# Two attentions and a feed-forward: maxima written in PSUM, work moved between the heads

## The chip, the cores and the metric

The kernel runs on one core of one Trainium2 chip as one program. The metric is the device time in microseconds from start to end of that program. The core has five engines with a queue of instructions each: TensorE (PE in the profile; its weight loads are PEld), VectorE (DVE), ScalarE (ACT), GpSimd (POOL) and SyncE (SP), which here only issues DMAs. They wait for each other by semaphores. TensorE writes to PSUM, a small memory of eight banks; the other engines read it from there into SBUF.

## The reference

Three stages follow each other, all in float32, with 4 batches, 576 positions and 512 features:

```python
# 1. attention with decay: 8 heads of 64 for each batch
cum = cumsum(log(clip(f, 1e-4, 1)), -1)
scores = q @ k.T / 8 + (cum[..., :, None] - cum[..., None, :])     # masked above the diagonal
attn = exp(scores - max(scores)); attn /= attn.sum(-1) + 1e-9
x = heads_side_by_side(attn @ v)                                   # (4, 576, 512)
# 2. mixing of positions by rank 32, and a feed-forward 512 -> 2048 -> 512
u = x + (x.T @ U @ V).T
y = u + relu(u @ w_ch1) @ w_ch2
# 3. four experts, each a masked attention of width 64; two of them count at each position
logits = y @ w_gate
w = softmax(the two largest logits)
out = sum over e of (w[e] if e is chosen else 0) * (softmax(causal((y wq[e]) (y wk[e]).T / 8)) @ (y wv[e]) @ wo[e])
```

## The kernel before

Nearly all products are made of a high and a low part: each operand is split into a rounded part (names that end in `h`, or `qa`, `ka`) and the rest (`l`, `qb`, `kb`), and three matmuls are added in PSUM. In the first attention a pair of heads shares its loads, so there are 16 pairs, four to a batch; the heads are counted 0 to 31 here. In the second attention a head is one expert of one batch, 0 to 15.

One head is made in these turns. `scores` (L186) makes the transposed scores in two parts, `sc`, each in a PSUM buffer of two banks; ScalarE takes the exponential into `pf` and a 16-bit `ph`, and VectorE the rest `pl`. So that the exponentials cannot overflow, the maximum of each row goes into the scores as an additional row of the matmul, and it is made before, for a later head: `row_max` (L148) has three turns. The first multiplies the last fifth of the rows, `ua`, and VectorE takes the masked maximum of 576 columns (L157), which adds the mask, writes the sum to `junk` in SBUF and the maximum to `mx`. The second does the same with the other four fifths, `ub` (448, 320, 192 and 64 columns, L175). `sc`, `ua` and `ub` share two buffers (tag `s2`). The third turn transposes the maxima on TensorE, `mt` (L180), VectorE scales them to `mr` (L182), and two DMAs on SP's queue write them into row 66 of `qa`. `weighted_values` makes `av` from `ph`, `pl` and the values, `normalise` scales it (L285). The values are scaled first by a power of two from their largest magnitude: `am` on VectorE (L249), `amt` on TensorE, `rsp`, `rs`.

The 16 tiles of the first two quarters of the feed-forward weights come in during the first attention. Each is a DMA, three steps on VectorE that narrow 64-bit numbers (L306, L308, L309, to `wst`), one on ScalarE between them (L307), the high part on ScalarE and the low part on GpSimd. `WRATE` says how many tiles are asked for behind each pair; their order on the engines is then set by the scheduler. `GROUPS` says how many pieces of feed-forward stand in each pair.

TensorE's order is written by hand: `first_batch` (the first four pairs), `later_batches` (the other twelve) and the loop of the second attention run turns of Python generators one after the other, `one(gen)` being one turn. The other engines' order comes from the scheduler. In the second attention the filling stands in a list `work` of generators, and `work_on(n)` takes n pieces from its front: `experts_qk` (projections of two experts: four pieces of 12 matmuls `pq`, L848), `expert_values` (five pieces of 12 matmuls `pv`, L891, then `am` and the scale, and the gates: `eq` and others on VectorE), `expert_out` (two pieces of transposes `op`, five of 6 matmuls `po`, L934) and `last_out` for the last batch. In a head stand, in this order: the first part of the scores, `ua` of the head after the next, one piece, the second part, one piece, `ub`, one piece, the weighted values of the head before, two pieces, `mt`, and in most heads another piece (none in the last batch but for its last head).

Of the kernel before, what the change touches and what calls it, by code (L numbers as in the profile page):

```python
# [8 lines left out]
F32 = mybir.dt.float32  # L9
# [8 lines left out]
P = 128  # L18
# [3 lines left out]
E = 4  # L22
# [13 lines left out]
PSCALE = 256.0  # L36
VEXP = 8192.0

WRATE = (0, 1, 2, 3, 3, 3, 2, 2)
GROUPS = (0,) * 5 + (6, 6, 7) + (8,) * 7 + (3,)  # L40
BIG = -1.0e30
NEG = -3.0e38
ISC = 0.125
# [13 lines left out]
def kernel(  # L57
# [90 lines left out]
    def row_max(hb, mx, apart=False):  # L148


        qa, qb, ka, kb = hb
        ua = ps2.tile([P, 2, 512], F32, name="ua", tag="s2")
        for c0, c1 in ((0, HC), (HC, S)):
            nc.tensor.matmul(ua[:, c0 // HC, 0:HC], qa[0:66, M_LO[4]:S], ka[0:66, c0:c1],
                             start=True, stop=True)
        junk = cur["att"].tile([P, S], BF16, name="junk", bufs=1)
        nc.vector.tensor_tensor_reduce(  # L157
            junk[:].rearrange("p (c n) -> p c n", c=2), ua[:, :, 0:HC],
            maskm[:].rearrange("p (c n) -> p c n", c=2), 1.0, NEG, OP.add, OP.max, mx[:, 4:5])
        if apart:  # L160
            yield
        ub = ps2.tile([P, 2, 512], F32, name="ub", tag="s2")
        where = {3: (0, 0), 0: (0, 448), 2: (1, 0), 1: (1, 320)}
        for t in (3, 2, 1, 0):
            bk, off = where[t]
            w = M_W[t]
            n = 64 if t == 0 else P
            nc.tensor.matmul(ub[0:n, bk, off:off + w], qa[0:66, M_LO[t]:M_LO[t] + n],  # L168
                             ka[0:66, 0:w], start=True, stop=True)
        for t in (3, 2, 1, 0):  # L170
            bk, off = where[t]
            w = M_W[t]
            n = 64 if t == 0 else P
            m0 = S - P if t == 0 else S - w
            nc.vector.tensor_tensor_reduce(  # L175
                junk[0:n, 0:w], ub[0:n, bk, off:off + w], maskm[0:n, m0:m0 + w], 1.0, NEG,
                OP.add, OP.max, mx[0:n, t:t + 1])
        yield
        mt = psf.tile([NT, P], F32, name="mt", tag="f")
        nc.tensor.transpose(mt[:], mx[:], ident[:])  # L180
        mr = small.tile([NT, P], F32R, name="mr", bufs=2)
        nc.vector.tensor_scalar(mr[:], mt[:], PSCALE_LN / ISC, None, OP.subtract)  # L182
        row = f32(qa[66:67, :])
        nc.sync.dma_start(row[:, 0:64], f32(mr[0:1, 0:64]))
        cur["last"] = nc.sync.dma_start(row[:, 64:S].rearrange("o (t p) -> o t p", p=P),
                                        f32(mr[1:NT, :]))  # L186
# [343 lines left out]
    def maxima(p, j, apart=False):  # L530
        if p < NPAIR:
            yield from row_max(pair_heads(p)[j], next_mx(), apart)

    def one(gen):

        next(gen, None)
# [104 lines left out]
    def pair_scores(p, j):  # L641
        st_p[p, j] = yield from scores(pair_heads(p)[j])

    def first_batch(m_next):

        mixing = vals = iter(())
        for h in range(2 * NP):
            p, j = divmod(h, 2)  # L650
            sc = pair_scores(p, j)
            one(sc)
            one(m_next)
            m_next = maxima(p + 1, j, True)
            one(m_next)
            if j == 0:
                xs[p] = sx.tile([P, NT, P], F32, name="x", bufs=2)
                vals = values(p + 1)
                one(vals)
            one(sc)  # L660
            if j == 1:
                next_inputs(p + 2)
            one(m_next)
            if j == 1:
                one(vals)
            if h > 0:
                attend(*divmod(h - 1, 2))
            if j == 0:
                one(vals)
                one(mixing)  # L670
            elif p > 0:
                mixing = mix(p - 1)
                one(mixing)
            if j == 1:
                weights_after(p)
        one(mixing)
        return m_next

    def later_batches(m1):

        m0 = iter(())
        for p in range(NP, NPAIR):
            some = [1] * GROUPS[p]

            def group():
                if some:
                    fill(some.pop())

            xs[p] = sx.tile([P, NT, P], F32, name="x", bufs=2)
            if p == NP:
                cur["att"] = att
            vals = values(p + 1)
            mixing = mix(p - 1)
            sc = pair_scores(p, 0)
            one(sc)
            group()
            one(m1)
            one(sc)  # L700
            group()
            m0 = maxima(p + 1, 0)
            one(m0)
            group()
            attend(p - 1, 1)
            one(vals)
            group()
            sc = pair_scores(p, 1)
            one(sc)
            one(vals)  # L710
            group()
            one(m0)
            one(mixing)
            one(sc)
            next_inputs(p + 2)
            group()
            one(mixing)
            if p == NP:
                sin0.release()
                att0.release()  # L720
                pre.release()
                cur["fu"] = pool("fu", 2, "right")
                cur["fh"] = pool("fh", 8, "right")
                cur["fy"] = pool("fy", 3, "right")
            if p % NP == 0:
                ffn_prepare(p - NP)
                if p == NP:
                    ffn_prepare(1)
            m1 = maxima(p + 1, 1)
            one(m1)  # L730
            one(vals)
            group()
            attend(p, 0)
            group()
            weights_after(p)
            fill(len(some))
        attend(NPAIR - 1, 1)
        fill(1)
        drain(mix(NPAIR - 1))
        ffn_prepare(NPAIR - NP)  # L740
# [232 lines left out]

    def expert_attend(b, e):
        if e == 0:
            st_o[b] = sy.tile([P, NT, E * D], F32, name="o3")
        vh, vl, rs, cf = st_v[b]
        ph, pl = st_e[b, e]
        av = weighted_values(ph, pl, vh[:, :, e], vl[:, :, e])
        rn = row_scales(av, rs, cf[:, e, :])  # L980
        normalise(st_o[b][:, :, e * D:e * D + D], av, rn)
# [9 lines left out]
    def work_on(n):  # L991

        while n and work:
            if next(work[0], 1) is None:
                n -= 1
            else:
                work.pop(0)

    NH = B * E
    with tc.manual_schedule(engines={mybir.EngineType.PE}):  # L1000
        drain(experts_qk(0, 0, y))
        work.append(experts_qk(0, 1, y))
        work_on(2)
        m0, m1 = head_max(0), head_max(1)
        one(m0)
        work_on(1)
        one(m0)
        work_on(1)
        one(m1)
        work.append(expert_values(0, y))  # L1010
        work_on(1)
        one(m1)
        work_on(1)
        one(m0)
        work_on(3)
        one(m1)
        y_next = load_y(1, ys[1], sy, "yst")
        for h in range(NH):
            b, e = divmod(h, E)
            more = b + 1 < B  # L1020
            if e == 0 and more:
                y = y_next
                work.append(experts_qk(b + 1, 0, y))
            if e == 1 and b + 2 < B:
                with tc.issue_after(cur["last"].ins):
                    y_next = load_y(b + 2, ys[b % 2], sy, "yst")
            if e == 1 and b > 0:
                work.append(expert_out(b - 1))
            if e == 2 and more:
                work.append(experts_qk(b + 1, 1, y))  # L1030
            if e == 3 and more:
                work.append(expert_values(b + 1, y))
            if e == 3 and not more:
                tail = last_out(b)
                work.append(tail)
            sc = expert_scores(b, e)
            m = head_max(h + 2) if h + 2 < NH else iter(())
            one(sc)
            one(m)
            work_on(1)  # L1040
            one(sc)
            work_on(1)
            one(m)
            work_on(1)
            if h > 0:
                expert_attend(*divmod(h - 1, E))
            work_on(2)
            one(m)
            if b == B - 1:
                work_on(e == 3)  # L1050
            elif e < 3:
                work_on(1)
        expert_attend(B - 1, E - 1)
        work_on(100)
    for p_ in (ys[1], sy, att, hpool2, hpool, sy0, sw, small, psf, ps1, ps2, dram, const):
# [58 lines left out]
```

## Time and profile before

| | |
|---|---|
| median of 3 runs | 966.55 us (965.96, 966.55, 969.4) |
| profiled execution | 971.0 us, its span 969.1 |
| TensorE busy | 862.1 us, 89% (7480 matmuls); weight loads 808.2 |
| VectorE busy | 568.4 us, 59% |
| ScalarE, GpSimd busy | 416.7 us, 293.5 us |
| granted TensorE clock, mean | 0.93 |
| moved by DMA | 101.94 MB |

The profile gives an engine's busy time in the whole span; the stages have different limits. TensorE is busy in nine tenths and more of nearly every slice between 130 and 720 us, where the feed-forward stands, and less at both ends. "Windows" cut the span into stretches and give each engine's busy time in them, and the clock that TensorE was granted, 1.00 being 2.4 GHz and 0.50 being 1.2 GHz. A wait in the profile is put down to the instruction that released it last.

### The profile page before, as it was taken

The page shows a single profiled execution, that of the slowest core. Times are in us where ns is not written, and L with a number is a line of the kernel's source. Part 1 is how long each engine was busy: PE and PEld are TensorE (multiplying, and loading weights), DVE is VectorE, ACT ScalarE, POOL GpSimd, SP SyncE. Part 2 cuts the span into 40 slices and gives each one's busy share as a digit, 9 for nine tenths or more (in the row PEclk, how much of TensorE's full clock was granted, in tenths as well). Part 3 has the DMA queues.
Part 4 walks back from the last instruction along what each step waited for, and adds up shares of the span by engine and source line. Part 5 has one row for each costly group of instructions (what it writes and reads, how often), then busy time and mean ns, then how long its engine had stood idle before and what let it go on. Part 6 is the DMA issues. An engine that isn't in the chain of part 4 may idle for free.

```text
span 969.1 us, 19020 instructions
## 1 busy us (share of the span) xinstructions
PE 862.1 (89%) x7480; PEld 808.2 (83%) x7480; DVE 568.4 (59%) x1468; ACT 416.7 (43%) x808; POOL 293.5 (30%) x262
## 2 busy tenths in 40 slices
PE   2769778878999998999999999999999797989887
PEld 2758667777899998989998999999999786878775
DVE  6787767776576665652246653222225778576654
ACT  4656446445545444441233342322113455545543
POOL 8444444433242223121225342423014132110000
PEclk9985559888999998999999999999999999999968
DMA  6344453335333232203158763423113213212111
GB/s 176 109 133 139 123 179 89 111 88 168 119 108 99 78 107 81 65 26 110 50 168 305 230 216 110 147 72 108 46 61 99 70 43 80 67 23 74 31 45 55
DMA packets 68777, 101.94 MB, mean 105 GB/s; under 512 B 6608, under 2 KB 49424, under 8 KB 68688
## 3 DMA queue, kind: packets, MB, share of 16 engines
q1 hardware_dynamic: 64416, 92.47, 32.6%
q10 hardware_dynamic: 4272, 8.26, 2.3%
q8 instruction: 59, 0.97, 0.4%
q14 instruction: 30, 0.25, 0.1%
HBM read 60.33 MB, written 22.56 MB: 86 GB/s over the span
## 4 chain that ended last, share of the span: by engine, by line
PE 68%; DVE 13%; DMA 8%; ACT 4%; issue 3%; POOL 2%; SPq 1%; ACTq 0%; POOLq 0%; DVEq 0%
PE cps L384 18%; PE hps L369 18%; PE sc L211 9%; PE pq L848 3%; PE po L934 3%; DMA ust<-udram 3%; PE pv L891 3%; PE av L238 3%; DVE pl L222 3%; PE ub L168 2%; PE gp L551 2%; PE av L242 2%; PE av L240 2%; DVE junk L175 2%; DMA vr<-in_v_dram 1%
## 5 line engine op out<-in xcount | busy, mean ns | idle before, releaser
L384 PE MATMUL cps<-hh,w2h 128*128 128x288 f32 x512 | 156.0, 305 | 5.2 <-DVE yc L386 3.9
L369 PE MATMUL hps<-uh,w1h 128*128 128x288 f32 x512 | 145.5, 305 | 8.8 <-ACT uh L354 8.8
L222 DVE TENSOR_TENSOR pl<-pf,ph 128x576 f16<-128x576 f32 x144 | 125.2, 874 | 47.0 <-ACT ph L221 46.7
L384 PE MATMUL cps<-hh,w2l 128*128 128x288 f32 x512 | 152.5, 298 | 0.0
L384 PE MATMUL cps<-hl,w2h 128*128 128x288 f32 x512 | 151.7, 296 | 0.0
L374 DVE SCALAR_TENSOR_TENSOR hl<-hps,hh 128x288 fp32r<-128x288 f32 x128 | 58.3, 455 | 145.7 <-ACT hh L373 145.4
L369 PE MATMUL hps<-uh,w1l 128*128 128x288 f32 x512 | 142.2, 299 | 0.0
L373 ACT ACTIVATE hh<-hps 128x288 fp32r<-128x288 f32 x128 | 52.4, 409 | 165.3 <-PE hps L369 165.0
L369 PEld LDWEIGHTS hps<-uh,w1h 128*128 128x128 f32 x512 | 98.0, 191 | 9.5 <-ACT uh L354 9.3
L220 ACT ACTIVATE pf<-sc 128x576 f32<-128x576 f32 x144 | 83.4, 612 | 47.9 <-PE sc L211 41.9
L384 PEld LDWEIGHTS cps<-hh,w2h 128*128 128x128 f32 x512 | 97.5, 191 | 6.5 <-DVE yc L386 4.6
L369 PEld LDWEIGHTS hps<-uh,w1l 128*128 128x128 f32 x512 | 98.2, 192 | 0.0
L384 PEld LDWEIGHTS cps<-hh,w2l 128*128 128x128 f32 x512 | 97.4, 190 | 0.0
L384 PEld LDWEIGHTS cps<-hl,w2h 128*128 128x128 f32 x512 | 97.3, 190 | 0.0
L238 PE MATMUL av<-vh,ph 128*128 128x65 f16 x720 | 92.8, 208 | 1.5 <-DVE x L285 1.5
L369 PE MATMUL hps<-ul,w1h 128*128 128x288 f32 x512 | 90.3, 299 | 3.3 <-POOL ul L355 3.3
L240 PE MATMUL av<-vl,ph 128*128 128x64 f16 x720 | 91.5, 204 | 0.0
L242 PE MATMUL av<-vh,pl 128*128 128x65 f16 x720 | 91.3, 204 | 0.0
L221 ACT CAST ph<-pf 128x576 f16<-128x576 f32 x144 | 88.5, 638 | 1.6
L211 PE MATMUL sc<-qa,ka 67*128 67x288 f32 (+4 forms) x288 | 81.2, 343 | 8.2 <-ACT pf L220 4.3
L175 DVE CUSTOM_DVE_ANT_0 junk<-ub,maskm 128x448 bf16<-128x448 f32 x192 | 79.7, 415 | 12.1 <-PE ub L168 10.7
L355 POOL TENSOR_TENSOR ul<-ust,uh 128x1152 fp32r<-128x1152 f32 x22 | 58.7, 2670 | 82.9 <-ACT uh L354 82.8
(160 smaller groups left out, 2002.4 us busy)
## 6 DMA issues: line engine op xcount, KB each, us to landing
raw<-in_w_dram SPq DMA_DIRECT2D x32, 512.0 KB
ust<-udram SPq DMA_DIRECT2D x22, 576.0 KB
qkt<-in_qk_dram SPq DMA_DIRECT2D x16, 576.0 KB
yc<-ydram SPq DMA_DIRECT2D x14, 576.0 KB
ydram<-yc SPq DMA_DIRECT2D x14, 576.0 KB
vr<-in_v_dram SPq DMA_DIRECT2D x16, 320.0 KB
udram<-ustage ACTq DMA_DIRECT2D x16, 288.0 KB
ydram<-ust SPq DMA_DIRECT2D x8, 576.0 KB
```

The lines of the kernel that those rows point to most:

```text
L175: nc.vector.tensor_tensor_reduce(junk[0:n, 0:w], ub[0:n, bk, off:off + w], maskm[0:n, m0:m0 + w], 1.0, NEG, OP.add, OP.max, mx[0:n, t:t + 1])
L211: nc.tensor.matmul(ps[:, bk, off:off + w], wa, xa, start=bk not in banks[:n], stop=bk not in banks[n + 1:])
L220: nc.scalar.activation(pfv, view, AF.Exp, scale=ISC)
L221: nc.scalar.copy(ph[:, o0:o0 + n], pf[:, 0:n])
L222: nc.vector.tensor_tensor(pl[:, o0:o0 + n], pf[:, 0:n], ph[:, o0:o0 + n], OP.subtract)
L238: nc.tensor.matmul(av[0:m, it, :], ph[0:k, c:c + m], vh[0:k, jt, :], start=first, stop=False)
L240: nc.tensor.matmul(av[0:m, it, 0:64], ph[0:k, c:c + m], vl[0:k, jt, :], start=False, stop=False)
L242: nc.tensor.matmul(av[0:m, it, :], pl[0:k, c:c + m], vh[0:k, jt, :], start=False, stop=last)
L355: nc.gpsimd.tensor_tensor(ul[:], ust[:], f32(uh[:]), OP.subtract)
L369: nc.tensor.matmul(ph[:], wa[:, k, fs], xa[:, k, :], start=n == 0, stop=n == 3 * KT - 1)
L374: nc.vector.scalar_tensor_tensor(hl[:], ph[:], 0.0, f32(hh[:]), OP.max, OP.subtract)
L384: nc.tensor.matmul(pc[:], wa[:, t, dsl], xa[:], start=n == 0, stop=n == 3 * FT - 1)
```

## The change

- The maxima's masked sums, which nothing reads, are written back to the place in PSUM that they are read from (`ua`, `ub`); the tile `junk` is gone.
- First attention, first batch: the third turn of the maxima (`mt`, `mr`, the row's DMAs) stands behind the second part of the scores and no longer in front of `ua`. In the other twelve pairs it stands behind the second part of the scores and a group of feed-forward in both heads, where it stood in front of the second part.
- The weights' tiles behind the pairs are 0, 0, 1, 4, 4, 4, 3 and not 0, 1, 2, 3, 3, 3, 2, 2.
- Second attention: the values of the next batch are put in the list in expert 1, not 3, the second half of the projections at the front of it in expert 2; the outputs of batches 0, 1 and 2 are put in from head 9 on, not one batch later each. How many pieces stand in front of `mt` in each head is in a table, `PIECES`, and behind `mt` none. The attention's results `o3` have three buffers, where they had two.

```diff
--- before.py
+++ after.py
@@ -36,8 +36,10 @@
 PSCALE = 256.0
 VEXP = 8192.0
 
-WRATE = (0, 1, 2, 3, 3, 3, 2, 2)
+WRATE = (0, 0, 1, 4, 4, 4, 3)
 GROUPS = (0,) * 5 + (6, 6, 7) + (8,) * 7 + (3,)
+
+PIECES = (3, 2, 2, 2) + (1,) * 4 + (3,) * 4 + (2, 2, 2, 3)
 BIG = -1.0e30
 NEG = -3.0e38
 ISC = 0.125
@@ -153,9 +155,8 @@
         for c0, c1 in ((0, HC), (HC, S)):
             nc.tensor.matmul(ua[:, c0 // HC, 0:HC], qa[0:66, M_LO[4]:S], ka[0:66, c0:c1],
                              start=True, stop=True)
-        junk = cur["att"].tile([P, S], BF16, name="junk", bufs=1)
         nc.vector.tensor_tensor_reduce(
-            junk[:].rearrange("p (c n) -> p c n", c=2), ua[:, :, 0:HC],
+            ua[:, :, 0:HC], ua[:, :, 0:HC],
             maskm[:].rearrange("p (c n) -> p c n", c=2), 1.0, NEG, OP.add, OP.max, mx[:, 4:5])
         if apart:
             yield
@@ -173,7 +174,7 @@
             n = 64 if t == 0 else P
             m0 = S - P if t == 0 else S - w
             nc.vector.tensor_tensor_reduce(
-                junk[0:n, 0:w], ub[0:n, bk, off:off + w], maskm[0:n, m0:m0 + w], 1.0, NEG,
+                ub[0:n, bk, off:off + w], ub[0:n, bk, off:off + w], maskm[0:n, m0:m0 + w], 1.0, NEG,
                 OP.add, OP.max, mx[0:n, t:t + 1])
         yield
         mt = psf.tile([NT, P], F32, name="mt", tag="f")
@@ -649,15 +650,15 @@
         for h in range(2 * NP):
             p, j = divmod(h, 2)
             sc = pair_scores(p, j)
+            m_last, m_next = m_next, maxima(p + 1, j, True)
             one(sc)
-            one(m_next)
-            m_next = maxima(p + 1, j, True)
             one(m_next)
             if j == 0:
                 xs[p] = sx.tile([P, NT, P], F32, name="x", bufs=2)
                 vals = values(p + 1)
                 one(vals)
             one(sc)
+            one(m_last)
             if j == 1:
                 next_inputs(p + 2)
             one(m_next)
@@ -696,9 +697,9 @@
             sc = pair_scores(p, 0)
             one(sc)
             group()
-            one(m1)
             one(sc)
             group()
+            one(m1)
             m0 = maxima(p + 1, 0)
             one(m0)
             group()
@@ -709,11 +710,11 @@
             one(sc)
             one(vals)
             group()
-            one(m0)
             one(mixing)
             one(sc)
             next_inputs(p + 2)
             group()
+            one(m0)
             one(mixing)
             if p == NP:
                 sin0.release()
@@ -973,7 +974,7 @@
 
     def expert_attend(b, e):
         if e == 0:
-            st_o[b] = sy.tile([P, NT, E * D], F32, name="o3")
+            st_o[b] = sy.tile([P, NT, E * D], F32, name="o3", bufs=3)
         vh, vl, rs, cf = st_v[b]
         ph, pl = st_e[b, e]
         av = weighted_values(ph, pl, vh[:, :, e], vl[:, :, e])
@@ -1024,12 +1025,14 @@
             if e == 1 and b + 2 < B:
                 with tc.issue_after(cur["last"].ins):
                     y_next = load_y(b + 2, ys[b % 2], sy, "yst")
-            if e == 1 and b > 0:
-                work.append(expert_out(b - 1))
+            if e == 1 and more:
+                work.append(expert_values(b + 1, y))
+            if e == 1 and b == 2:
+                work.append(expert_out(0))
+            if e < 2 and b == 3:
+                work.append(expert_out(1 + e))
             if e == 2 and more:
-                work.append(experts_qk(b + 1, 1, y))
-            if e == 3 and more:
-                work.append(expert_values(b + 1, y))
+                work.insert(0, experts_qk(b + 1, 1, y))
             if e == 3 and not more:
                 tail = last_out(b)
                 work.append(tail)
@@ -1044,12 +1047,9 @@
             work_on(1)
             if h > 0:
                 expert_attend(*divmod(h - 1, E))
-            work_on(2)
+
+            work_on(PIECES[h])
             one(m)
-            if b == B - 1:
-                work_on(e == 3)
-            elif e < 3:
-                work_on(1)
         expert_attend(B - 1, E - 1)
         work_on(100)
     for p_ in (ys[1], sy, att, hpool2, hpool, sy0, sw, small, psf, ps1, ps2, dram, const):
```

TensorE in head 0 of the first attention, from the end of the first part of the scores on; `identb` and `maskt` are the causal mask. Before:

```order
L211 LDWEIGHTS identb
L211 MATMUL sc<-maskt,identb 128x128
L180 MATMUL mt<-ident,mx_96 5x128 [waits DVE_49]
L154 MATMUL ua<-ka_154,qa_152 128x288 [waits Activation_49]
L154 MATMUL ua<-ka_154,qa_152 128x288
L211 MATMUL sc<-qa_136,ka_138 128x320 [waits Activation_49]
```

and with the change, the same place and the end of the second part:

```order
L212 LDWEIGHTS identb
L212 MATMUL sc<-maskt,identb 128x128
L156 MATMUL ua<-ka_154,qa_152 128x288 [waits DVE_49,Activation_49]
L156 MATMUL ua<-ka_154,qa_152 128x288
L212 MATMUL sc<-qa_136,ka_138 128x320 [waits Activation_49]
...
L212 MATMUL sc<-maskt,identb 128x128
L181 MATMUL mt<-ident,mx_96 5x128
L169 MATMUL ub<-ka_154,qa_152 128x448 [waits DVE_49]
```

`mt` has moved behind the ten matmuls and four masks of the second part and waits for nothing of its own; the wait for VectorE stands at `ua`.

VectorE in head 4 of the first attention, where `wst` is a weight's tile, `g` the mixing, `am` the values' magnitude and `den` a head's sums. Before:

```order
L306 TENSOR_SCALAR wst<-raw 128x512
L555 TENSOR_TENSOR g<-gp,g 32x128
L182 TENSOR_SCALAR mr<-mt 5x128
L157 ISA junk,mx_98<-ua,maskm 128x576
L157 ISA mx_98 128x1
L308 SCALAR_TENSOR_TENSOR wst<-raw,wst 128x512
L222 TENSOR_TENSOR pl<-pf,ph 128x576
L309 SCALAR_TENSOR_TENSOR wst<-raw,wst 128x512
L249 TENSOR_REDUCE am<-vr 128x1
L175 ISA junk,mx_98<-ub,maskm 128x448
```

and with the change:

```order
L286 TENSOR_TENSOR x<-av,rn 128x5x64
L556 TENSOR_TENSOR g<-gp,g 32x128
L158 ISA ua,mx_98<-ua,maskm 128x2x288
L158 ISA mx_98 128x1
L223 TENSOR_TENSOR pl<-pf,ph 128x576
L183 TENSOR_SCALAR mr<-mt 5x128
L176 ISA ub,mx_98<-ub,maskm 128x448
```

The three `wst` steps are gone from between the maxima, `mr` stands behind the maximum of `ua`, and `am` (in the next rows) behind the first maximum of `ub`.

TensorE in head 12 of the second attention, from the end of its weighted values on. Before:

```order
L240 MATMUL av<-vl_10785,ph 128x64
L242 LDWEIGHTS pl
L242 MATMUL av<-vh_10784,pl 128x65
L180 MATMUL mt<-ident,mx_98 5x128
L211 MATMUL sc<-qa_8040,ka_8042 128x288
```

and with the change:

```order
L935 MATMUL po<-wol,oh 128x512
L935 MATMUL po<-woh,ol 128x512
L935 MATMUL po<-woh,oh 128x512
L935 MATMUL po<-wol,oh 128x512
L935 MATMUL po<-woh,ol 128x512
L181 MATMUL mt<-ident,mx_98 5x128
L212 MATMUL sc<-qa_8008,ka_8010 128x288
```

Output products (two pieces of six matmuls, the end of which is shown) now stand between the weighted values and `mt`, where nothing stood.

## Rows read from the trace of the kernel before

**Rows 1.** Windows, first attention; columns: length, busy time (instructions), granted clock, DMA.

```profile
18.97:40.73 21.76, 14.60 (x95) 12.79 (x96) 16.07 (x40) 12.73 (x23) 10.70 (x11) 1.00 0.46 132
40.73:46.46 5.73, 5.51 (x74) 4.98 (x72) 4.70 (x16) 4.07 (x8) 3.73 (x3) 1.00 0.02 5
46.46:64.69 18.23, 14.29 (x163) 12.33 (x160) 14.31 (x40) 10.68 (x19) 10.66 (x7) 0.91 0.61 183
64.69:79.62 14.93, 10.58 (x82) 9.30 (x81) 13.33 (x37) 8.79 (x16) 6.16 (x6) 0.67 0.37 106
79.62:90.54 10.92, 10.14 (x79) 9.07 (x78) 7.79 (x25) 6.37 (x12) 5.45 (x4) 0.52 0.39 109
90.54:105.57 15.03, 11.24 (x88) 9.58 (x87) 12.56 (x29) 8.12 (x15) 5.76 (x4) 0.71 0.61 180
105.57:130.78 25.21, 22.27 (x158) 18.86 (x158) 15.87 (x41) 14.24 (x26) 9.51 (x7) 0.50 0.44 119
```

**Rows 2.** Waits from 0 to 170 us; columns: total us, times, longest us.

```profile
PE mt L180 <- DVE mx L175: 11.1, 4, 4.4
```

**Rows 3.** Timeline of VectorE, head 4; columns: start, length in us, engine, line.

```profile
63.75 1.90 DVE L309 SCALAR_TENSOR_TENSOR wst<-raw,wst 128x512 int32<-128x512 int32 x1
```

**Rows 4.** Timeline of VectorE and PE at the first head's row of maxima.

```profile
16.23 0.27 DVE L182 TENSOR_SCALAR mr<-mt 5x128 fp32r<-5x128 f32 x1
...
18.97 0.58 PE L211 MATMUL sc<-qa,ka 67*128 67x288 f32 x1 [2.28 <-DMA qa<-mr]
```

**Rows 5.** Windows, second attention: heads 0 to 3, 4-11, 12, 13, 14, tail.

```profile
754.21:769.42 15.21, 10.05 (x65) 9.18 (x63) 13.65 (x37) 6.77 (x13) 3.42 (x3) 0.89 0.05 10
769.42:776.61 7.19, 6.34 (x82) 5.88 (x82) 5.50 (x18) 5.72 (x14) 1.34 (x2) 1.00 0.92 250
776.61:788.60 11.99, 11.25 (x118) 10.66 (x118) 10.16 (x27) 7.44 (x18) 6.23 (x7) 1.00 0.13 28
788.60:800.41 11.81, 11.81 (x133) 11.50 (x130) 7.16 (x22) 5.64 (x12) 0.00 (x0) 1.00 0.18 39
800.41:912.08 111.67, 100.71 (x952) 91.39 (x949) 75.97 (x220) 57.20 (x120) 13.07 (x14) 0.95 0.22 60
912.08:923.41 11.33, 5.30 (x74) 4.52 (x72) 10.64 (x30) 5.29 (x9) 3.00 (x1) 0.83 0.00 0
923.41:939.64 16.23, 16.23 (x98) 13.32 (x98) 8.35 (x30) 5.85 (x12) 0.00 (x0) 0.59 0.05 18
939.64:946.07 6.43, 6.43 (x77) 5.24 (x75) 1.73 (x3) 5.10 (x9) 0.00 (x0) 1.00 0.34 125
946.07:969.00 22.93, 16.27 (x153) 12.22 (x149) 10.83 (x25) 7.57 (x15) 0.00 (x0) 0.89 0.18 58
```

**Rows 6.** Waits from 745 to 969 us.

```profile
PE mt L180 <- DVE mx L175: 12.8, 5, 5.1
...
PE pq L848 <- DVE mr L182: 2.6, 3, 0.9
```

**Rows 7.** VectorE's groups by form: count | busy us, mean ns | idle before.

```profile
L157 DVE CUSTOM_DVE_ANT_0 junk<-ua,maskm 128x576 bf16<-128x576 f32 x48 | 36.1, 753 | 22.1 <-PE ua L154 21.5
...
L309 DVE SCALAR_TENSOR_TENSOR wst<-raw,wst 128x512 int32<-128x512 int32 x32 | 29.4, 920 | 0.4
...
L306 DVE TENSOR_SCALAR wst<-raw 128x512 int32<-128x512 int32 x32 | 19.3, 604 | 20.7 <-POOL w2l L344 10.1 <-DMA raw<-in_w_dram 5.9 <-POOL w1l L344 4.6
...
L175 DVE CUSTOM_DVE_ANT_0 junk<-ub,maskm 64x64 bf16<-64x64 f32 x48 | 10.1, 210 | 0.3
...
L249 DVE TENSOR_REDUCE am<-vr 128x1 f32<-128x1280 f32 x4 | 5.9, 1486 | 0.1
```

**Rows 8.** Chain of waits around 740 and 950 us: start, length in us.

```profile
730.99 9.54 PE pq L848 x72
...
746.47 1.45 PE pv L891 x12
...
950.31 1.44 PE po L934 x6
```

## Prediction

> **What bounds the kernel now.** I read the 40 slices of the page first, for where PE is idle or short of clock: at both ends of the program; between them the feed-forward matmuls keep PE full and little of the change reaches there. So I cut both ends into heads, 0 to 31 in the first attention and 0 to 15 in the second, each from its first score matmul to the next head's, and read their windows, then the waits in them. In a window's row the reader is to compare PE's and VectorE's busy time with the length, and to see the granted clock.
>
> First attention, first batch (8 heads) and the pair after it: 111.8 us for ten heads (21.76 + 5.73 + 18.23 + 14.93 + 10.92 + 15.03 + 25.21 [rows 1]). Head 2 takes 5.73 us at full clock with PE and VectorE both nearly full; heads 3 and 4 take 18.23, head 5 14.93, head 6 10.92, head 7 15.03. The clock is 0.91 in heads 3 and 4, 0.67 in head 5 and 0.52, 0.71 and 0.50 after it. What stops PE is `mt`, the transpose of the maxima: 11.1 us in four waits, the longest 4.4 [rows 2], always for the last masked maximum on VectorE. VectorE is late because weight-narrowing work stands between the maxima, and that work stretches: the same instruction takes 1.90 us at the start of head 4 [rows 3] and 0.92 in the mean of 32 [rows 7], so it is not the instruction's own rate but something beside it (GpSimd is busy for 10.66 of the 18.23 us of heads 3 and 4).
>
> Second attention: 214.8 us for 16 heads with the tail (15.21 + 7.19 + 11.99 + 11.81 + 111.67 + 11.33 + 16.23 + 6.43 + 22.93 [rows 5]). Head 3, with five value pieces to fill PE, has it busy 11.81 of 11.81 us; head 12, with no piece, has PE busy 5.30 of 11.33 us and VectorE 10.64, and head 13 behind it gets a clock of 0.59: its 16.23 us are 16.23 x 0.59 = 9.6 us of full-clock work. Again `mt` waits for the last maximum: 12.8 us in five waits, the longest 5.1, and the next projection waits for `mr` behind it, 2.6 us in three [rows 6].
>
> **The change part by part.**
> *`mt` behind the second scores (first attention).* This step I expect to give little by itself. The scores and both maxima tiles share two PSUM buffers, and `ua` takes the buffer that `ub` held; `mt` and `ua` both wait for the same last maximum. In the order of PE the wait moves from `mt` to `ua` and `mt` is left without one. So of the 11.1 us nothing goes but the transpose and `mr` that stood between the maximum and `ua`: about 0.5 us in each of the heads that wait. What it adds is a later row: the row of maxima must land before the next head's scores, and in the one place where it is last, the first head, those scores start at 18.97 us, 2.47 us after `mr` ended at 16.50 (16.23 + 0.27), with 2.28 us of PE idle [rows 4]. After the change `mt` stands behind the second scores; behind it only `ub`, the weighted values and half a mix cover the row: at full clock some 0.6 + 1.7 + 1.0 = 3.3 us (an estimate from head 2, whose whole PE time of 5.51 us holds scores, maxima and values), and the row needs about 0.5 + 0.27 + 2.47 = 3.2 us. The two are level, so I count a head of the first batch as 7.0 us at full clock, not 5.73. SP's queue holds the next pair's copies around it; they are ahead in both kernels.
>
> *Weights 0, 0, 1, 4, 4, 4, 3 in place of 0, 1, 2, 3, 3, 3, 2, 2.* All 16 tiles remain. The order of VectorE shows no narrowing at all in heads 2 to 5 and one tile in head 6, where now heads 4 to 7 hold it. That removes what made PE wait. Heads 2 to 7 take 64.84 us now (5.73 + 18.23 + 14.93 + 10.92 + 15.03). With the clock full throughout they would take 6 x 7.0 = 42; with it at half from head 3 on, a head costs head 6's busy PE time, 10.14 us at 0.52, so 6.5 + 5 x 10.5 = 59. Both ends are open because the clock falls after such waits and in these heads does not come back by itself (0.50 through the pair behind head 7, though PE is busy 22.27 of 25.21 us). I take 53, nearer the half-clock end, since that is what rows 1 show for most of this stretch: -11.8. Heads 0 and 1 lose part of their 4.4 us wait because one of the two `vst` steps moves behind the last maximum: 21.76 becomes 20.1, -1.7. The tiles come back later: one more in the pair behind the batch (+1.0), one more in each of the next three pairs and two fewer in the fourth. A tile is three VectorE steps, L306 of 0.60 us, L309 of 0.92 [rows 7] and L308, the same operation on the same shape, taken alike: 2.4 us; behind the batch VectorE is busy 15.87 of 25.21 us, so under half of it shows, in the next pairs I count it whole: +7.2 - 4.8 = +2.4, between -5 and +7. First attention: -11.8 - 1.7 + 1.0 + 2.4 = -10.1.
>
> *Maxima written into PSUM.* 240 instructions keep their count and lengths, and only the place of a result that nobody reads changes. Into SBUF they take 753 ns for 576 columns and 210 for 64 [rows 7]: 1.06 ns a column, and 0.14 us fixed; no row shows VectorE writing PSUM. Bounds: the fixed part gone, 5 x 0.14 = -0.7 us a head, and twice the column time, 1600 columns x 1.06 = +1.7 us a head. I take 0, the rate of those rows, and keep the upper end as a rival. The Trainium skill speaks against this step ("Perfetto Trace Analysis", Optimizing Scalar/DVE Operations): it puts the fixed access cost of a VectorE instruction at about 60 ns on SBUF and 125 ns on PSUM; no run here shows it for a write. If the write pays the difference, an estimate by that page is 5 x 0.065 = 0.33 us a head, and over the 22 heads in which VectorE is last 7 us of the gain would be lost.
>
> *Second attention's pieces.* The work is the same; its place is new. A projection piece of 12 matmuls costs 9.54 / 6 = 1.59 us, a value piece 1.45, an output piece of 6 1.44 [rows 8]. By head, from the order of PE:
> Head 0: the third projection piece moves from behind `mt` to in front of it. It now runs while the maximum is awaited, so 1.59, the 0.9 wait for `mr` and most of the clock's loss (10.05 x 0.11 = 1.1, counted as 0.9) go: 15.21 - 3.4 = 11.8. Head 1 gets four value pieces: busy 6.34 + 5.8 = 12.1. Head 2 gets one: 11.25 + 1.45, with a little wait 13.0. Head 3 loses all filling and becomes what head 12 is now, with the same VectorE order (the gates' steps `amt`, `rsp` and `eq` in front of the last maximum): 11.3. Together 48.2 against 46.2 now (15.21 + 7.19 + 11.99 + 11.81).
> Heads 4 to 7: head 4 is head 2's present row, 12.0, plus half-clock matmuls behind head 3's wait: 0 to 6.6 (head 13's excess, 16.23 - 9.6), I take 3.0, as its filling is dense projections. Head 5: 11.81 - 1.45 = 10.4. Head 6: 12.0. Head 7 has one value piece, and `am` (1.49 us [rows 7]), the scale and `vr` in front of its last maximum: between 6.1 (PE alone) and 12.8 (head 12 plus a piece), taken 10.2. Together 47.6.
> Heads 8 to 11: 12.5; 11.8 + 2.2, as `amt` now stands straight behind the last value piece and waits for its copy and `am`; 12.0; and 14.0 for head 11, whose outputs' `ol` stand behind `eq`. Together 52.5, and heads 4 to 11 100.1 against 111.67.
> Heads 12 to 14: full-clock work now 5.30 x 0.83 + 9.6 + 6.43 = 20.4, plus 36 output matmuls (6 x 1.44 = 8.6) and one set of transposes (about 1): 30.0 against 33.99 (11.33 + 16.23 + 6.43); the low clock goes because every head has filling. Tail: the same order, 22.9. A third `o3` buffer is what lets outputs wait; DMAs of the outputs go out in the last two batches where the DMA share is now 0.34 at most [rows 5].
> Sum 48.2 + 100.1 + 30.0 + 22.9 = 201.2 against 214.8: -13.6.
>
> **The sum.** -10.1 - 13.6 = -23.7 on the profiled execution's 971.0 us (span 969.1): 947. Its own run stood 4.4 us above the median 966.55, so the time is 966.55 - 23.7 = 943.
>
> **The rivals.**
> Both clocks hold. Heads 2 to 7 take 42 instead of 53 (-11 more): 932. For it: the order has no stall left there but the row. Against: the clock of 0.50 to 0.71 in rows 1.
> The waits only change their name in the first batch. `ua` inherits `mt`'s wait, rows are late, and 59 or more us remain for heads 2 to 7, with the later pairs at their upper bound (+7): -5.8 - 1.7 + 1.0 + 7 = 0.5 in the first attention in place of -10.1, 953.
> Head 12's stall comes four times. Heads 3, 7 and 11 each end in a gates wait and drag a half-clock head behind them as head 12 does now, 6.6 us each: 3 x 6.6 less the 3.0 counted = +17: 960.
> Slower: the PSUM write. If VectorE reads and writes one PSUM bank at half rate, every head costs 1.7 us more where VectorE is last: ten heads at the start, eight in the four pairs behind, four at the gates: 22 x 1.7 = +37, so 980. It decides from +1.1 us a head (23.7 / 22), that is when the 576-column maximum goes from 753 ns to over about 1.1 us. Nothing in the rows excludes it; for the plain rate speaks only that the instruction already streams PSUM at one column a cycle.
>
> **How the numbers follow.** Forecast 943 +-6: 0.40. Both clocks hold: 0.17. Waits renamed: 0.18. Four stalls: 0.13. PSUM write: 0.08. The rest, 0.04, lies above. Two of ten are left out by 926 to 963; the forecast's own range is 937 to 949. What the measurement can tell from no change is about 0.5%, 961.7 to 971.4. Faster: all but the last two cases and a third of the four stalls, 0.83; same 0.07; slower 0.10.
>
> **What would show it.** In the profile after: `mt` waits for nothing in the first attention and `ua` (in later pairs the second scores) takes the wait; heads 2 to 7 of the first batch hold no narrowing and take 42 to 59 us; the clock of those heads and of the pair behind them is above 0.6; head 3 of the second attention takes about 11 us and heads 12 to 14 about 30 at full clock; the 576-column maximum stays near 753 ns. Wrong if the maxima are longer by 0.2 us or more, if PE's waits for the row (`sc` for the DMA of `mr`) pass 5 us in sum, or if heads 4, 8 and 12 run at half clock.

## The result and the profile after

The changed kernel takes 940.62 us (937.89 to 943.63 in 4 runs) against 967.35 before: ratio 0.9723, 95% interval 0.9693 to 0.9754, so 26.7 us less. The forecast was 943, in 926 to 963. The profiled run has a span of 939.0 us.

The windows of the first attention after the change, cut as in [rows 1] (heads 0 and 1, 2, 3 and 4, 5, 6, 7, 8 and 9) with one row more for heads 10 to 17; columns: length, busy time of PE, PEld, VectorE, ScalarE, GpSimd, granted clock, DMA share, GB/s:

```profile
19.60:39.62 20.02, 14.80 (x96) 12.81 (x96) 16.03 (x44) 13.08 (x23) 9.95 (x11) 1.00 0.51 140
39.62:47.66 8.04, 7.89 (x70) 7.08 (x71) 4.50 (x14) 4.57 (x8) 5.58 (x4) 1.00 0.28 71
47.66:62.43 14.77, 12.44 (x159) 10.85 (x158) 13.67 (x46) 10.84 (x20) 7.44 (x5) 1.00 0.43 116
62.43:69.43 7.00, 6.32 (x80) 5.57 (x81) 6.57 (x26) 5.03 (x9) 1.41 (x1) 1.00 0.30 86
69.43:76.71 7.28, 5.98 (x78) 5.24 (x78) 6.96 (x19) 5.32 (x11) 2.77 (x2) 1.00 0.72 197
76.71:92.96 16.25, 8.29 (x88) 7.02 (x88) 14.14 (x33) 8.88 (x16) 9.17 (x6) 0.83 0.54 151
92.96:118.67 25.71, 22.19 (x158) 18.94 (x158) 14.05 (x41) 13.66 (x26) 9.68 (x7) 0.50 0.49 136
118.67:236.24 117.57, 104.15 (x953) 94.73 (x953) 94.44 (x235) 65.53 (x122) 55.19 (x36) 0.89 0.47 141
```

The same heads 10 to 17 in the kernel before:

```profile
130.78:259.09 128.31, 105.23 (x956) 97.48 (x954) 91.89 (x228) 62.55 (x116) 49.29 (x32) 0.87 0.40 116
```

Heads 2 to 6 run at full clock, 37.1 us (8.04 + 14.77 + 7.00 + 7.28), where they took 49.8 in [rows 1] and 47.7 in e1, a kernel below with the same first attention as before. Head 7 is the long one now: 16.25 us, half of it without PE. The clock falls there, and is 0.50 through heads 8 and 9, though PE is busy 22.19 of 25.71 us. What PE waits for in head 7 is the mixing's `g`, which stands on VectorE behind a weight's tile. VectorE in that stretch, then PE's wait, then GpSimd (columns: start, length, engine, line; in brackets the idle time before):

```profile
85.52 1.48 DVE L307 TENSOR_SCALAR wst<-raw 128x512 int32<-128x512 int32 x1
86.92 1.83 DVE L223 TENSOR_TENSOR pl<-pf,ph 128x512 f16<-128x512 f32 x1
...
88.81 1.75 DVE L309 SCALAR_TENSOR_TENSOR wst<-raw,wst 128x512 int32<-128x512 int32 x1
...
90.69 0.28 DVE L556 TENSOR_TENSOR g<-gp,g 32x128 fp32r<-32x128 f32 x1
```
```profile
91.03 0.58 PE L561 MATMUL up<-vs,g 96*128 96x256 f32 x1 [7.21 <-DVE g L556]
```
```profile
84.98 1.73 POOL L521 TENSOR_TENSOR qb<-qkt,qb 64x576 fp32r<-64x576 f32 x1
86.79 1.41 POOL L271 TENSOR_TENSOR vl<-vr,vh 128x640 f16<-128x640 f32 x1
88.28 1.73 POOL L522 TENSOR_TENSOR kb<-qkt,kb 64x576 fp32r<-64x576 f32 x1
```

The tile is not the whole of it. L307, `pl` and L309 take 1.48, 1.83 and 1.75 us here; in the same trace they take 0.42, 0.68 and 0.69 where GpSimd does nothing beside them. Each of the three begins while a GpSimd step runs and ends 0.3 to 0.6 us behind it. That is 3.3 of the 7.2 us.

PE's waits from 0 to 170 us, by releaser (total, times, longest; `up` is the mixing's second product, `cps` the feed-forward's), answer [rows 2]: `mt` is not among them any more, and the row of maxima (`qa<-mr`) is, with 5.5 us in place of one wait of 2.28:

```profile
PE up L561 <- DVE g L556: 7.2, 1, 7.2
...
PE sc L212 <- DMA qa<-mr: 5.5, 4, 3.1
...
PE cps L385 <- ACT w2h L344: 2.0, 1, 2.0
```

The second attention, cut as in [rows 5]:

```profile
732.91:745.48 12.57, 8.49 (x65) 7.78 (x63) 11.68 (x30) 7.17 (x14) 3.44 (x3) 1.00 0.07 14
745.48:759.05 13.57, 13.57 (x130) 13.23 (x130) 9.69 (x28) 8.20 (x20) 5.09 (x7) 0.87 0.48 133
759.05:771.48 12.43, 12.43 (x133) 12.09 (x130) 8.87 (x25) 6.72 (x15) 1.51 (x2) 1.00 0.12 25
771.48:783.43 11.95, 5.29 (x74) 4.51 (x72) 11.29 (x31) 5.42 (x10) 3.56 (x3) 0.87 0.17 37
783.43:882.75 99.32, 90.88 (x904) 84.67 (x903) 74.82 (x223) 51.31 (x109) 12.67 (x12) 0.95 0.20 48
882.75:895.20 12.45, 10.79 (x100) 8.39 (x98) 6.97 (x22) 6.19 (x13) 0.00 (x0) 1.00 0.17 54
895.20:906.21 11.01, 10.43 (x100) 8.31 (x98) 7.00 (x21) 6.87 (x13) 0.00 (x0) 1.00 0.32 110
906.21:916.99 10.78, 10.78 (x94) 8.72 (x94) 3.85 (x10) 6.00 (x11) 0.00 (x0) 1.00 0.21 75
916.99:939.00 22.01, 16.30 (x148) 12.00 (x146) 9.21 (x20) 8.02 (x16) 0.00 (x0) 0.89 0.22 73
```

It is 8.7 us shorter (206.1 for 214.8). Head 3 is what head 12 was (PE 5.29 of 11.95 us), and the low clock that stood behind head 12 is gone there; heads 12 to 14 all have output products now. `mt` still waits in this stage, three times for 11.0 us, where it waited five times for 12.8 us in [rows 6]:

```profile
PE mt L181 <- DVE rn L280: 5.2, 1, 5.2
PE mt L181 <- DVE qb L864: 3.1, 1, 3.1
PE mt L181 <- DVE rn L282: 2.7, 1, 2.7
```

The steps named there stand behind the last maximum on VectorE, so the names mislead. The longest wait is head 3's. In front of its last maximum stands the gates' `eq`, 2.56 us long beside a GpSimd step, where two of the four `eq` take 0.23:

```profile
779.79 3.00 POOL L271 TENSOR_TENSOR vl<-vr,vh 128x1280 f16<-128x1280 f32 x1 [7.60 <-ACT vh L270]
780.32 2.56 DVE L819 TENSOR_TENSOR eq<-eq,tie 128x80 f32<-128x80 f32 x1
783.03 0.17 DVE L280 RECIPROCAL rn<-den 128x5 f32<-128x5 f32 x1
```

The maxima, by form (count | busy us, mean ns), against [rows 7]: the two sums shown are 6 and 9 ns longer (16 at 448 columns). The instruction that reads the accumulator out behind each maximum takes 135 ns, and took 81; the second fence is the kernel before.

```profile
L158 DVE CUSTOM_DVE_ANT_0 ua<-ua,maskm 128x576 f32<-128x576 f32 x48 | 36.4, 759 | 14.4 <-PE ua L156 14.3
...
L176 DVE DVE_READ_ACCUMULATOR2_ANT mx<- 128x1 f32 x144 | 19.5, 135 | 0.1
...
L176 DVE CUSTOM_DVE_ANT_0 ub<-ub,maskm 64x64 f32<-64x64 f32 x48 | 10.5, 219 | 0.2
```
```profile
L175 DVE DVE_READ_ACCUMULATOR2_ANT mx<- 128x1 f32 x144 | 11.7, 81 | 0.0
```

### The profile page after: what moved, and what is told of

Same layout as the page of the kernel before. It is cut to its first block, busy times and chain, and to the rows that moved or that the text cites. A ratio compares the mean times of both kernels' runs of the same rounds, so it can differ in the third digit from the quotient of the medians.

```text
span 939.0 us, 18998 instructions
## 1 busy us (share of the span) xinstructions
PE 847.3 (90%) x7480; PEld 792.6 (84%) x7480; DVE 562.3 (60%) x1468; ACT 415.3 (44%) x808; POOL 294.1 (31%) x262
## 4 chain that ended last, share of the span: by engine, by line
PE 70%; DVE 14%; DMA 6%; ACT 5%; issue 3%; POOL 1%; SPq 1%; POOLq 0%; ACTq 0%; DVEq 0%
PE cps L385 19%; PE hps L370 19%; PE sc L212 8%; PE pq L849 4%; PE po L935 3%; PE pv L892 3%; PE av L239 3%; DVE pl L223 2%; DMA ust<-udram 2%; PE ub L169 2%; DVE ub L176 2%; PE gp L552 2%; PE av L243 2%; PE av L241 2%; PE ua L156 1%
## 5 line engine op out<-in xcount | busy, mean ns | idle before, releaser
L223 DVE TENSOR_TENSOR pl<-pf,ph 128x576 f16<-128x576 f32 x144 | 121.6, 847 | 54.4 <-ACT ph L222 54.2
L212 PE MATMUL sc<-qa,ka 67*128 67x288 f32 (+4 forms) x288 | 79.1, 334 | 14.6 <-DMA qa<-mr 5.5
L239 PE MATMUL av<-vh,ph 128*128 128x65 f16 x720 | 86.4, 202 | 1.5 <-DVE x L286 1.5
L176 DVE CUSTOM_DVE_ANT_0 ub<-ub,maskm 128x448 f32<-128x448 f32 x192 | 81.4, 424 | 7.2 <-PE ub L169 6.0
L241 PE MATMUL av<-vl,ph 128*128 128x64 f16 x720 | 85.1, 198 | 0.0
L243 PE MATMUL av<-vh,pl 128*128 128x65 f16 x720 | 84.8, 198 | 0.0
```

Of the source, the lines that this page charges most:

```text
L176: nc.vector.tensor_tensor_reduce(ub[0:n, bk, off:off + w], ub[0:n, bk, off:off + w], maskm[0:n, m0:m0 + w], 1.0, NEG, OP.add, OP.max, mx[0 ...
L212: nc.tensor.matmul(ps[:, bk, off:off + w], wa, xa, start=bk not in banks[:n], stop=bk not in banks[n + 1:])
L223: nc.vector.tensor_tensor(pl[:, o0:o0 + n], pf[:, 0:n], ph[:, o0:o0 + n], OP.subtract)
L239: nc.tensor.matmul(av[0:m, it, :], ph[0:k, c:c + m], vh[0:k, jt, :], start=first, stop=False)
L241: nc.tensor.matmul(av[0:m, it, 0:64], ph[0:k, c:c + m], vl[0:k, jt, :], start=False, stop=False)
L243: nc.tensor.matmul(av[0:m, it, :], pl[0:k, c:c + m], vh[0:k, jt, :], start=False, stop=last)
```

## The experiments

Each ratio is to the kernel before, run beside it (966 to 968 us), with its 95% interval. A single profile's stretch is a weak witness in the first attention: e1 has the first attention of the kernel before, instruction for instruction on every engine, and its profile reaches the second attention at 744.7 us and not at 754.2. So the medians decide, and a stretch counts where several kernels agree on it.

**e1, the second attention's part alone** (`PIECES`, the list, three `o3` buffers).

> Only the second attention's part of the change (table of pieces, values and projections earlier, outputs in the last two batches, three o3 buffers). The traces give 8.7 us less from the first score matmul of the second attention to the end (214.8 to 206.1). Theory A, the parts add up: 9 to 12 us faster (the rest being the cost of the PSUM writes in these 16 heads, 16 x 0.31 us at most), ratio about 0.990. Theory B, the parts need each other (the earlier pieces only pay with a shorter maximum): under 5 us.

959.63 us, ratio 0.9931 (0.9900 to 0.9963): 7 us. Between the two theories; the interval, 4 to 10 us, excludes neither.

**e2, the first attention's turns and rates alone**, with `junk` in SBUF.

> Only the turns of the maxima and the weights' rates of the first attention; maxima still written to junk in SBUF, second attention as before. The traces give 21.3 us less up to the second attention. Theory A: 20 to 25 us faster, ratio about 0.977. Theory B (the place of the maxima's result matters for the first attention): under 15 us.

959.54 us, ratio 0.9926 (0.9903 to 0.9950): 7 us. The time of Theory B, and a surprise: nearly all of the gain was to come from here. Whether it is the place of the result, as Theory B has it, e5 and e6 decide.

**e3, the place of the sums alone.**

> Only the place of the maxima's masked sums: PSUM in place of junk. In the trace after, a maximum's own instruction is 6 to 16 ns longer than before and the accumulator read behind it 55 ns (81 to 136), 0.31 us a head. Theory A: the longer reads are on the path where VectorE is last, 22 heads: 0 to 7 us slower, 4 taken. Theory B: they are hidden or a buffer less makes up for it: within 1 us of before.

963.85 us, ratio 0.9965 (0.9940 to 0.9990): not slower, if anything 3 us faster. Neither theory: the reads are 136 ns here too. But more than the place is new: at least 152 of VectorE's 1468 instructions stand elsewhere in its order than in the kernel before, so the 3 us cannot be put down to the place.

**e4, the changed kernel with the sums in SBUF.**

> The changed kernel with junk in SBUF again. Theory A: 2 to 6 us faster than the changed kernel, about 936 (ratio to before 0.967), accumulator reads back at 81 ns. Theory B: level with the changed kernel, 940, because the reads stand where VectorE has time.

948.93 us, ratio 0.9822 (0.9788 to 0.9856): 8 us slower than the changed kernel, the wrong way for both theories. Its PE waits in head 16 for the last weights, and e2's does just the same (waits from 200 to 245 us in e4; `cps` is the feed-forward's second product, `w2h` and `w2l` the two parts of a weight's tile):

```profile
PE cps L386 <- ACT w2h L345: 4.5, 1, 4.5
...
PE cps L386 <- POOL w2l L346: 1.7, 2, 1.0
```

The maxima are not slower in e4 (750 ns for 576 columns, 80 for the read). But its order is another: the scheduler, which places everything but TensorE's work, put at least 142 of VectorE's 1468 instructions elsewhere when the result's place changed. That made two theories, and two kernels that cross them:

**e5 and e6, place and order crossed.** The edit gives four engines an order from a table, by edges that add no wait. In the traces e6 has VectorE's order of e4, and e5 that of the changed kernel but for two maxima with their reads:

```diff
+ORDER = {"DVE": ("0 2 1 ..."), "Activation": (...), "Pool": (...), "SP": (...)}
...
+            for _a, _b in zip(_ns, _ns[1:]):
+                tc.add_manual_dep(_all[_b], _all[_a].name, ... NoSync ..., reason="order")
```

> Maxima's sums in SBUF (junk) as in e4, but VectorE, ScalarE, GpSimd and SyncE in the order that they have in the changed kernel (on VectorE all but two maxima). Theory O, the 8 us between e4 (949) and the changed kernel (941) are the order, which came out otherwise: 937 to 942, with accumulator reads of 80 ns. Theory P, they are the place itself (SBUF written beside other work): about 949.

> The mirror of e5: maxima's sums in PSUM as in the changed kernel, the four engines in the order of e4. Theory O: 947 to 953, the last weights late as in e4 (the second product of head 16 waits 4 us and more for them). Theory P: about 941.

| | order of the changed kernel | order of e4 |
|---|---|---|
| sums in PSUM | 940.62 (0.9723) | e6: 947.36 (0.9805, 0.9766 to 0.9845) |
| sums in SBUF | e5: 941.00 (0.9743, 0.9709 to 0.9776) | e4: 948.93 (0.9822) |

Theory O: the columns differ by 7 to 8 us, the rows by nothing that can be told. Head 16, in e5 and then in e6 (windows, columns as above), shows where:

```profile
209.86:222.23 12.37, 11.38 (x124) 10.79 (x120) 10.92 (x27) 7.25 (x13) 6.88 (x4) 1.00 0.53 171
```
```profile
209.89:230.49 20.60, 14.33 (x117) 12.81 (x118) 14.71 (x37) 7.79 (x14) 6.77 (x5) 0.83 0.41 117
```

Both reach head 16 at 209.9 us; in e6 the last tiles are late there, and 8 us are gone.

**e7, the weights' rates alone**, and **e8, the turns alone.**

> Only the weights' rates (0, 0, 1, 4, 4, 4, 3); maxima's turns as before, junk in SBUF. Theory A, the rates alone empty heads 2 to 7 (VectorE has no narrowing there) and the turns are worth little: heads 2 to 7 take 54 to 57 us, all together 4 to 7 us faster than before, nearly e2. Theory B, the turns are needed: heads 2 to 7 over 60, no gain.

> Only the turns: mt, mr and the row behind the second part of the scores, in all 16 pairs; rates as before. Theory A, the wait moves to ua in the first batch and only the later pairs gain: heads 2 to 7 take 60 to 65 us, 0 to 4 us faster. Theory B, the turns carry the gain: heads 2 to 7 under 57 and 6 us or more faster.

e7: 944.13 us, ratio 0.9779 (0.9742 to 0.9817), 22 us faster. e8: 952.25, ratio 0.9850 (0.9810 to 0.9890), 14.5. Both are far outside Theory A's times (4 to 7 and 0 to 4 us), and both are better alone than together (e2, 7 us). In e7 and e2, heads 10 to 15 and then head 16:

```profile
116.62:207.20 90.58, 74.63 (x705) 68.87 (x702) 73.56 (x176) 51.05 (x95) 46.10 (x29) 0.89 0.49 146
207.20:218.91 11.71, 11.48 (x123) 10.74 (x120) 11.53 (x30) 7.17 (x14) 5.77 (x4) 1.00 0.53 150
```
```profile
118.10:207.94 89.84, 74.81 (x700) 68.25 (x700) 69.43 (x169) 50.08 (x93) 43.92 (x28) 0.89 0.49 142
207.94:229.94 22.00, 15.70 (x117) 14.12 (x118) 14.61 (x39) 7.86 (x15) 6.77 (x5) 0.77 0.36 107
```

They come to head 16 together, 20 us sooner than before (227.4) and 12 sooner than e1 (220.0), and e2 gives 10 of them back there. Heads 2 to 7 take 57.2 us in e7, 61.2 in e8 and 54.4 in e2 (64.8 before, 60.8 in e1), so for that stretch Theory A of e8 holds (60 to 65) and e7's upper end; what neither theory saw is that the later pairs gain more than it. In e8, with the turns alone, heads 10 to 15 take 87.0 us, where they took 96.6 before and 95.7 in e1.

**e9, rates and second attention, no turns, sums in SBUF**, and **e10, e9 with another table**:

```diff
-PIECES = (3, 2, 2, 2) + (1,) * 4 + (3,) * 4 + (2, 2, 2, 3)
+PIECES = (4, 1, 1, 1) + (1,) * 4 + (3,) * 4 + (2, 2, 2, 3)
```

> The weights' rates and the second attention's part, without the turns of the first attention and with junk in SBUF. Theory A: the two stages add up, since the first attention's order is that of e7: 944.1 less the 9.2 us by which e4's second attention is shorter than e7's (208.8 to 199.6): 935. Theory B: they do not (as turns and rates did not): over 940.

> e9 with the table's first four entries 4, 1, 1, 1 in place of 3, 2, 2, 2: the first batch's heads then hold what the second batch's hold, one piece of values left in head 3. In the traces heads 4 to 7 (9 pieces in heads 5 to 7) take 32.4 us for heads 5 to 7 where heads 1 to 3 (10 pieces) take 38. Theory A, the stall of head 3 and the low clock around it cost those 4 us: heads 0 to 3 together 46 to 48 in place of 50, and the kernel 2 to 4 us faster than e9. Theory B, the stall moves to head 4 whole: level with e9.

e9: 933.26 us, ratio 0.9641 (0.9608 to 0.9675). Theory A: where the first attention's order stays (it is e7's, instruction for instruction), the stages add up. e10: 931.24 us, ratio 0.9628 (0.9598 to 0.9659); the 2 us to e9 are inside the intervals. Its heads 0 to 3 take 47.4 us, as Theory A had it (52.8 in e9), with PE full in heads 1 and 2:

```profile
727.75:742.83 15.08, 11.10 (x78) 10.34 (x75) 13.67 (x37) 7.54 (x15) 3.38 (x3) 0.92 0.10 22
742.83:753.69 10.86, 10.86 (x120) 10.50 (x118) 6.71 (x21) 7.01 (x17) 1.62 (x3) 0.95 0.56 152
753.69:764.68 10.99, 10.99 (x120) 10.63 (x118) 7.73 (x21) 6.76 (x16) 5.08 (x6) 1.00 0.13 28
764.68:775.12 10.44, 6.61 (x86) 5.94 (x84) 9.88 (x35) 5.46 (x10) 0.56 (x2) 0.98 0.20 43
```

e10 beats both kernels, the changed one by 9 us.

**e11, turns and rates, tiles asked for earlier**: e2 with `WRATE = (0, 0, 2, 4, 4, 4, 2)`.

> e2 (turns and weights' rates, junk in SBUF, second attention as before) with rates 0, 0, 2, 4, 4, 4, 2, that is every tile from the second on asked for one place earlier. Theory A, what turns and rates together lose against either alone is the last tiles, on which the second product of head 16 waits 4.5 us and more: head 16 takes 12 to 14 us, not 22, heads 10 to 17 about 117, and the kernel about 951, 8 us less than e2. Theory B, it is the order at large: within 3 us of e2 (959.5).

962.25 us, ratio 0.9946 (0.9921 to 0.9971). Theory A fell: head 16 takes 22.1 us, and the last tile's first step on VectorE begins at 226.95 us (224.4 in e2). It is Theory B: VectorE's order is that of e2, instruction for instruction, and with the order left as it was the earlier request brought no tile earlier.

**e12, e10 with the turns moved in the first batch alone.**

> e10 with the turns moved in the first batch alone (mt behind the second part of the scores in heads 0 to 7; later pairs as before). It splits what turns and rates lose together. Theory A, the loss comes from the turns of the later pairs, which put the last weights' tiles later in VectorE's order: here head 16 takes about 12 us, heads 0 and 1 take 20 in place of 22, and the kernel is at 928 to 932, level with e10 or up to 3 us faster. Theory B, it comes from the turns of the first batch: head 16 takes over 18, the start of the second attention is 10 us later than in e10 (727.8), the kernel over 938.

940.77 us, ratio 0.9713 (0.9675 to 0.9750), 9.5 us slower than e10. Theory A fell; the time is Theory B's, but not the place: head 16 takes 14.3 us, and it is reached at 214.3 us where e10 reaches it at 205.6. With the turns moved in eight heads the tiles come later all along (the eighth begins on VectorE at 149.8 us, in e10 at 139.1), and in heads 10 and 11 PE waits 8.2 us for the feed-forward's first input (5.7 in e10) and 2.9 for parts of a tile (none in e10).

## Why the prediction was right, and where it was not

The time was right (943 forecast, 940.6 measured), and so were side and range. That it came so close is luck in part: the sum came out of two terms that missed on opposite sides. The first attention was to give 10.1 us; by the medians, if the parts add, it gave some 19.5 (26.7 less e1's 7.2), and between the two profiles 21.3, up to 9.5 of them the scatter that e1 shows. The second attention was to give 13.6 and gave 7 to 9.

- *Heads 0 to 7.* Forecast 20.1 for heads 0 and 1 and 53 for 2 to 7; measured 20.0 and 53.3. The total is right by another road: I had half clock from head 3 on, but five heads run at full clock, 7.4 us each, near the 7.0 of the rival in which both clocks hold, and one head (7) takes 16.25 us, for a tile that I had counted as no stall and for three steps held up beside GpSimd. Heads 2 to 7 were to hold no narrowing; heads 6 and 7 begin a tile each. That `ua` would inherit `mt`'s wait is half right: `mt`'s 11.1 us are gone, `ua` waits for VectorE for only 1.2 us (0.7 and 0.5), and the row came up as foreseen, to 5.5 us, just over the 5 that I had named as a warning.
- *Heads 8 and 9.* +1.0 forecast, +0.5 measured, at half clock as before, though I had looked for a clock above 0.6.
- *The tiles that come back later: the step that failed.* "+2.4, between -5 and +7" for heads 10 to 17; the profiles show -10.7, and -8.0 against e1's profile, outside these bounds both times. VectorE's narrowing there did grow by about that, 31.1 us for 28.9 (39 steps for 30). But I took PE's waits to stay, and for the turns behind the first batch I counted nothing ("I expect to give little by itself"). In heads 10 to 15 PE waits for `mt` for 7.2 us in the kernel before, in the longer of two waits behind a narrowing step of 1.83 us, and for 7.5 us in e1; in the changed kernel not at all. In head 16 what decides is whether VectorE's order lets the last tiles through before the head's product asks for them. e2, e4, e6 and e11 have the one bad order (head 16 20.6 to 22.1 us), the changed kernel, e5, e7 and e10 a good one (11.7 to 12.4); before it took 17.9, in e1 16.1, in e8 16.5. The wait for `mt` in the kernel before, heads 10 to 15 (130.78 to 227.4 us):

```profile
PE mt L180 <- DVE mx L175: 7.2, 2, 4.9
```

- *Maxima in PSUM.* Taken at 0; a maximum costs 54 ns more in its read, and 5 to 16 ns in itself, 0.31 us a head. That is near the price worked out from the Trainium skill ("Perfetto Trace Analysis", Optimizing Scalar/DVE Operations: 125 less 60 ns, an estimate of 0.33 us a head); the trace agrees, and shows most of it in the read. In the time it is within the noise (e5 against the changed kernel). The 7 us that could follow did not, and the slower rival is refuted: 759 ns, not over 1.1 us. Yet the edit mattered by 8 us as a change of order (e5, e6), a road that no case of the prediction had.
- *Second attention.* -13.6 forecast, -8.7 in the profile, -7 by e1. Heads 0 to 3 took 50.5 us for 48.2: head 1 has PE full and a clock of 0.87. Heads 4 to 11 came as forecast in sum, 99.3 for 100.1, and the stalls of heads 3, 7 and 11 did not each drag a half-clock head behind them (0.85, 0.77 and 1.00 in heads 4, 8 and 12). Heads 12 to 14 took 34.2 for 30.0: PE's busy time alone is 32.0, 2 more than the sum of full-clock work, and 2.2 us of waits (1.5 for `ol`, 0.7 for `pf`) had no term.

The parts are worth 7 (e1), 7 (e2) and 3 us (e3) alone and 27 together. Of the 10 us between, e4 to e6 show 7 to 8 to be order; the rest is within the intervals. Which instruction's place on VectorE it is that delays the tiles when turns and rates come together is not settled: e11 shows that the request alone changes nothing, e12 that the first batch's turns alone delay tiles, but without the long head 16, and no run moved one instruction alone.

## What to carry to other kernels

Where a scheduler places part of the work, an edit is two edits, the one in the diff and the new order: compare the orders before pricing the diff, and to tell them apart run the new code in the old order and the old code in the new. Price work that another engine has a deadline for by the deadline, not by its busy time. Where a step takes longer than its like, look at what the other engines do beside it. And of several changes that go in together, time each alone: here two of them were worth more without each other, and the fastest kernels (e9, e10) have neither the moved turns nor the sums in PSUM.

## What the runs showed of the hardware

- The accumulator's read after a VectorE maximum takes 135 ns when the maximum's sum goes to PSUM and 81 when it goes to SBUF (136 in e3, 80 in e5), and the sum itself takes 1 to 4% more (759 for 753 ns, 219 for 210).
- After head 7's wait of 7.2 us the granted clock stays at 0.50 through 25.7 us in which PE is busy for 22.2.
- What stretches the narrowing steps, after the change as in [rows 3], is GpSimd: the traces settle it. The 14 profiles hold 896 of the two narrowing steps that take two operands from SBUF (L309 and L310, 128x512). 766 of them take 0.64 to 0.70 us, and the other 130 take 0.78 to 3.02. Each of the 130 begins while a GpSimd instruction runs and ends 0.54 to 0.56 us behind that instruction. Of the 766, 703 have no GpSimd instruction beside them, in 42 one begins during the step, 15 begin in the last 0.11 us of one, and in six GpSimd began only 0.07 to 0.14 us before VectorE; in these six GpSimd's step took longer, 2.04 to 2.09 us for 1.41. The 576-column maxima, which read PSUM, take 743 to 767 ns with GpSimd busy beside them or not.
